# Causal scores in quarters: three 64 by 64 blocks per head in place of one 128 by 128, masked in two operations

## The chip, the cores and the metric

The kernel runs on one core of one Trainium2 chip. The core has TensorE (PE, matmuls; its weight loads are listed as PEld), VectorE (DVE), ScalarE (ACT), GpSimd (POOL) and SyncE (SP, which here issues the loads), and 16 DMA engines. The metric is the device time of one execution in microseconds, the median of several runs; lower is better.

## The reference

Retention attention (a linear attention with a decay per head) followed by a mixture of experts with one expert per token. Cut to what matters:

```python
# q, k, v: (4, 8, 768, 64)
gamma = 1.0 - 2.0 ** (-5.0 - np.arange(H))
for t in range(S):
    state = gamma * state + outer(k[t], v[t])        # per batch and head
    y[t] = scale * q[t] @ state
x = y as (B * S, H * D)                              # (3072, 512)
e_idx = argmax(x @ w_gate); gate_w = its softmax probability
eom = sigmoid(x @ w_output_gate)
out[token] = gate_w * eom[e_idx] * (relu(x @ w1[e_idx]) @ w2[e_idx])
```

Position t sees positions up to t only. Within a chunk of 128 positions the kernel computes this as scores of all keys with all queries, set to zero where the key is later than the query.

## The kernel before

The work has two parts. The first (about 0 to 155 us) is attention, routing and a scatter of the token rows to a list sorted by expert; the second runs the experts' two layers on TensorE to the end. The change lies in the first.

A sequence of 768 positions is cut into 6 chunks of 128; two chunks are a pair, so the 4 sequences give 12 pairs (`NPR`), j = 0 to 11, 3 to a sequence (`NJ`). The 8 heads are taken two by two: 4 groups (`NG`), and in each the even head lies on the lower 64 partitions and the odd head on the upper 64 (`LO`, `HI`, `half`). The order of the work is the order in which it is written: a loop over j (line 693) whose body calls small functions, each of which issues instructions on one or two engines; every engine takes its own in that order. For one pair the TensorE stages come in this order:

- `scores(j)` (line 336): for each of the two chunks c a PSUM tile `w` (two banks, one per head of a group; two such tiles take turns) receives keys by queries, 4 groups x 2 heads = 8 fp32 matmuls of 64 by 128 by 128. VectorE multiplies it with the 0/1 `mask` into `am` (line 346) in SBUF.
- `inter(j)` (L360): what the queries take from the state of earlier chunks, added up in the two banks `py`. Its matmuls lie on quarters of 64 by 64 of the array. For the first chunk of a sequence there is no state, and half of them fall away.
- `logits(j - 1)` (L394), `turn_k(j + 1)` (L311, transposes of the next keys into a `w` tile), `turn_l(j - 1)` (L402).
- `attend(j, 0)` (L367): values times `am` of the first chunk, into `py`; `weigh(j, 0)` (L374, VectorE) takes it out of PSUM. `state` (L383) updates the running state.
- `turn_q(j + 1)` (L329), `tokens(j - 1)` (L490), `counts(j - 1)` (L452 to L459), then `attend(j, 1)`, `weigh(j, 1)` and `state(j + 1, 0)`, and the next pair's scores.

Queries are stored with even positions of a chunk first and odd ones behind: column r x 64 + t of a query tile is position 2t + r (r = 0, 1). So positions 0 to 63, the early queries, are columns t = 0 to 31 of both halves, and the late ones t = 32 to 63. Keys are in plain order, partition p is position p.

In the profile each fp32 matmul shows as two LDWEIGHTS and two MATMUL records.

Of the kernel before, what the change touches and what calls it, by code (L numbers as in the profile page):

```python
# [10 lines left out]
F32 = mybir.dt.float32  # L11
# [5 lines left out]
ALU = mybir.AluOpType  # L17
# [15 lines left out]
def retention_moe_kernel(  # L33
# [14 lines left out]
    nc = tc.nc  # L48
    P = 128
# [5 lines left out]
    NG = H // 2  # L55
# [18 lines left out]
    mask = cpool.tile([P, 2, 64], F32, name="mask")  # L74
# [128 lines left out]
    with tc.manual_schedule(engines=None), ExitStack() as actx:  # L203
        ac = actx.enter_context(tc.tile_pool(name="ac", bufs=1))
        ap = actx.enter_context(tc.tile_pool(name="ap", bufs=2))
# [5 lines left out]
        qt, kt, vs, qr, ams, yts, sd, rt = {}, {}, {}, {}, {}, {}, {}, {}  # L211
        LO, HI = slice(0, 64), slice(64, 128)
        half = (LO, HI)

        def load2(which, src, tag, j, bufs):
            b, jb = divmod(j, NJ)
            t = ap.tile([P, 2, H, D], F32, name=tag, tag=tag, bufs=bufs)
            for c in range(2):
                r0 = (2 * jb + c) * P
                nc.sync.dma_start(t[:, c], src[b, :, r0:r0 + P, :].rearrange("h p d -> p h d"))  # L220
            which[j] = t

        def load_q(j):
            b, jb = divmod(j, NJ)
            t = ap.tile([P, H, 2, D], F32, name="qn", tag="qn", bufs=2)
            nc.sync.dma_start(t, q[b, :, jb * 2 * P:(jb + 1) * 2 * P, :].rearrange("h (p r) d -> p h r d", r=2))
            qn[j] = t
# [8 lines left out]
        gc = ac.tile([P, 2, NC, NG], F32, name="gc")  # L236
        wg = ac.tile([P, 2, NG, 32], F32, name="wg")
        gv = ac.tile([P, NC, H], F32, name="gv")

        load_q(0)  # L240
        load2(kn, k, "kn", 0, 3)
        load2(vn, v, "vn", 0, 2)
        nc.gpsimd.memset(wg, 0.0)
        nc.scalar.dma_start(gv, dec_v)
        load_q(1)
        for n, h in enumerate(half):
# [45 lines left out]
        def wide():  # L292
            return ps_w.tile([P, 2, 512], F32, name="w", tag="w")
# [24 lines left out]
        def turn_q(j, halved=False, tags=()):  # L318
# [14 lines left out]
                nc.scalar.copy(o.rearrange("p g c t -> p (g c t)"), w.rearrange("p b x -> p (b x)"))  # L333
            qt[j] = o

        def scores(j, between=None):
            for c in range(2):
                if c and between:
                    between()
                w = wide()  # L340
                for g in range(NG):
                    for hh in range(2):
                        nc.tensor.matmul(w[:, hh, g * P:(g + 1) * P], kt[j][half[hh], c, g], qt[j][half[hh], g, c],  # L343
                                         start=True, stop=True)
                a = ap.tile([P, 2, NG, P], F32, name="am", tag="am", bufs=2)
                nc.vector.tensor_tensor(  # L346
                    out=a.rearrange("p b g t -> p (b g) t"), in0=w.rearrange("p b (g t) -> p (b g) t", g=NG),
                    in1=mask.rearrange("p r t -> p (r t)").unsqueeze(1).broadcast_to([P, 2 * NG, P]), op=ALU.mult)
                ams[c] = a

        def open_y():
            rt["py"] = [ps_1.tile([P, 512], F32, name="py", tag=f"y{c}") for c in range(2)]
# [319 lines left out]
        load_pair(2)  # L672
        open_y()
        scores(0)
        prep_q(1, nc.vector)
        state(0, 0)
# [16 lines left out]
        for j in range(1, NPR - 1):  # L693
# [11 lines left out]
            if j >= 2 and j - 2 != EARLY:  # L705
                scatter(j - 2, 0)
            open_y()
            scores(j, (lambda: state(1, 0)) if j == 1 else None)
            if j - 1 in w_at:
                cast_weights(w_at[j - 1])  # L710
# [38 lines left out]
        j = NPR - 1  # L749
        scatter(j - 2, 0)  # L750
        scatter(j - 2, 1)
        open_y()
        scores(j)
        inter(j)
        logits(j - 1)
# [60 lines left out]
    with tc.manual_schedule(engines=None), ExitStack() as mctx:  # L816
# [197 lines left out]
        for s in range(NS + 1):  # L1014
            e, f = divmod(s, NF)
# [31 lines left out]
    with tc.If(odd > 0):  # L1047
        with ExitStack() as octx:
            oc = octx.enter_context(tc.tile_pool(name="oc", bufs=1))
            op = octx.enter_context(tc.tile_pool(name="op", bufs=2))  # L1050
# [49 lines left out]
            rows = oc.tile([P, 1], I32, name="rows")  # L1100
# [71 lines left out]
```

## Time and profile before

| | us |
|---|---|
| median of 3 runs (434.22 to 435.75) | 434.37 |
| the profiled execution's own time | 434.43 |
| its span, first to last instruction | 432.6 |
| TensorE busy | 413.7 (96%) |
| VectorE busy | 265.4 (61%) |
| ScalarE busy | 179.2 (41%) |
| GpSimd busy | 187.3 (43%) |
| the 24 mask operations, L346, 1219 ns each | 28.3 |

A row of a timeline gives the start, the length and the engine of instructions of the same kind that follow each other, then the line, the operation, what it writes and reads, and how many there are (x32). For matmuls "64*128" is the part of the array, rows by columns, and "64x128" what is streamed: partitions by columns. In brackets stands how long the engine stood idle before and what ended that. The end of a matmul is modelled, so the times between starts are the ones to use. A row of a window gives an engine's busy time in the stretch, its instructions in parentheses, and TensorE's granted clock as a share of full speed.

### The profile page before, as it was taken

What the parts mean: (1) busy time and instruction counts of PE and PEld (TensorE: products, weight loads), DVE (VectorE), ACT (ScalarE), POOL (GpSimd) and SP (SyncE); (2) the same over time, 40 slices, a digit from 0 to 9 for tenths busy, and PEclk for the clock granted to TensorE, in tenths of its full rate; (3) what the DMA queues carried; (4) which work ended last, traced back from release to release, by engine and by line L of the source; (5) the groups of instructions that cost most, each with busy time, mean ns of one, the idle gap of its engine ahead of it and who ended that gap; (6) DMA issues with size and microseconds to landing.
All of it is one profiled execution on the core that took longest, in us unless ns stands there. A gap on an engine that the chain in (4) does not pass through costs nothing.

```text
span 432.6 us, 10297 instructions
## 1 busy us (share of the span) xinstructions
PE 413.7 (96%) x3696; PEld 394.4 (91%) x3696; DVE 265.4 (61%) x701; ACT 179.2 (41%) x392; POOL 187.3 (43%) x255
## 2 busy tenths in 40 slices
PE   8799989999999999999999999999999999999990
PEld 5689878999979999999999999999999999999990
DVE  2667778677898757846456655664665756664110
ACT  2144454556546325544334443433444544441111
POOL 5446647666644216440025424524523533432522
PEclk9989999999999999999999999999999999999997
DMA  9999999999282498893394485558448549520102
GB/s 194 203 216 240 265 231 225 275 263 248 78 264 83 120 221 254 254 232 99 98 233 134 135 191 169 167 155 198 145 142 214 176 125 231 157 91 13 38 19 73
DMA packets 126878, 74.33 MB, mean 172 GB/s; under 512 B 56872, under 2 KB 115116, under 8 KB 126816
## 3 DMA queue, kind: packets, MB, share of 16 engines
q1 hardware_dynamic: 119888, 59.58, 54.9%
q0 software_dynamic: 5728, 13.93, 9.5%
q8 instruction: 31, 0.51, 0.5%
q10 hardware_dynamic: 1200, 0.06, 0.2%
q14 instruction: 31, 0.25, 0.2%
HBM read 59.62 MB, written 15.23 MB: 173 GB/s over the span
## 4 chain that ended last, share of the span: by engine, by line
PE 52%; issue 7%; POOL 3%; POOLq 0%; DVE 0%
PE h L875 26%; PE a L893 26%; POOL out_dram L178 3%; POOLq L178 0%; POOLq L1046 0%; DVE hl L880 0%; DVE a L1013 0%
## 5 line engine op out<-in xcount | busy, mean ns | idle before, releaser
L178 POOL DMA_INDIRECT out_dram<-ot,idi x83 | 87.2, 1050 | 150.4 <-ACT hh L879 123.2
L893 PE MATMUL a<-hh,whi 128*128 128x192 f32 (+7 forms) x256 | 85.6, 334 | 0.5 <-DVE a L1013 0.5
L893 PE MATMUL a<-hl,whi 128*128 128x192 f32 (+7 forms) x256 | 85.8, 335 | 0.1
L875 PE MATMUL h<-xh,whi 128*128 128x192 f32 (+7 forms) x256 | 85.7, 335 | 0.0
L875 PE MATMUL h<-xh,wlo 128*128 128x192 f32 (+7 forms) x256 | 85.7, 335 | 0.0
L875 PE MATMUL h<-xw,whi 128*128 128x192 f32 (+7 forms) x256 | 85.6, 335 | 0.0
L893 PE MATMUL a<-hh,wlo 128*128 128x192 f32 (+7 forms) x256 | 85.5, 334 | 0.0
L880 DVE SCALAR_TENSOR_TENSOR hl<-h,hh 128x192 fp32r<-128x192 f32 (+7 forms) x64 | 34.7, 544 | 63.9 <-ACT hh L879 63.8
L879 ACT ACTIVATE hh<-h 128x192 fp32r<-128x192 f32 (+7 forms) x64 | 30.8, 481 | 85.7 <-PE h L875 85.7
L165 DVE TENSOR_TENSOR wlo<-raw,whi 128x512 fp32r<-128x512 f32 x64 | 43.9, 686 | 30.1 <-ACT whi L160 28.7
L160 ACT CAST whi<-raw 128x512 fp32r<-128x512 f32 x64 | 39.6, 619 | 38.6 <-PE a L893 35.7
L893 PEld LDWEIGHTS a<-hh,whi 128*128 128x128 f32 x256 | 48.2, 188 | 1.1 <-ACT hh L879 0.7
L893 PEld LDWEIGHTS a<-hl,whi 128*128 128x128 f32 x256 | 48.2, 188 | 0.8 <-DVE hl L880 0.3
L875 PEld LDWEIGHTS h<-xh,wlo 128*128 128x128 f32 x256 | 48.2, 188 | 0.4
L875 PEld LDWEIGHTS h<-xh,whi 128*128 128x128 f32 x256 | 48.2, 188 | 0.4
L875 PEld LDWEIGHTS h<-xw,whi 128*128 128x128 f32 x256 | 48.2, 188 | 0.4
L893 PEld LDWEIGHTS a<-hh,wlo 128*128 128x128 f32 x256 | 48.2, 188 | 0.4
L166 DVE TENSOR_TENSOR wlo<-raw,whi 128x512 fp32r<-128x512 f32 x64 | 43.9, 685 | 0.3 <-ACT whi L160 0.3
L161 ACT CAST whi<-raw 128x512 fp32r<-128x512 f32 x64 | 39.5, 617 | 0.0
L346 DVE TENSOR_TENSOR am<-w,mask 128x1024 f32<-128x1024 f32 x24 | 28.3, 1219 | 6.7 <-PE w L343 6.6
L514 POOL DMA_INDIRECT srt<-row,posi x24 | 24.7, 1031 | 16.2 <-issue 5.2
L853 ACT CAST xh<-xt 128x416 fp32r<-128x416 f32 (+3 forms) x32 | 16.2, 510 | 37.0 <-DVE xt L852 37.0
(170 smaller groups left out, 610.9 us busy)
## 6 DMA issues: line engine op xcount, KB each, us to landing
raw<-in_moe_w_dram SPq DMA_DIRECT2D x128, 256.0 KB, 3.3
qn<-in_q_dram SPq DMA_DIRECT2D x12, 512.0 KB, 6.1
kn<-in_k_dram SPq DMA_DIRECT2D x24, 256.0 KB, 5.6
vn<-in_v_dram SPq DMA_DIRECT2D x24, 256.0 KB, 6.2
xl<-srt SPq DMA_DIRECT2D x12, 211.2 KB, 5.3
xl<-srt SPq DMA_DIRECT2D x12, 195.0 KB, 4.9
out_dram<-ot,idi POOLq DMA_INDIRECT x83, 2.6
xl<-srt SPq DMA_DIRECT2D x4, 227.5 KB, 6.9
```

The costliest lines, as they stand in the source:

```text
L160: nc.scalar.copy(hi[:, 0], raw[:, 0])
L161: nc.scalar.copy(perm(hi), r2)
L165: nc.vector.tensor_sub(lo[:, 0], raw[:, 0], hi[:, 0].bitcast(F32))
L166: nc.vector.tensor_sub(perm(lo), r2, perm(hi).bitcast(F32))
L178: st = nc.gpsimd.indirect_dma_start(out=dst, out_offset=bass.IndirectOffsetOnAxis(ap=idx, axis=0), in_=src, in_offset=None, bounds_check=n ...
L346: nc.vector.tensor_tensor(out=a.rearrange("p b g t -> p (b g) t"), in0=w.rearrange("p b (g t) -> p (b g) t", g=NG), in1=mask.rearrange("p ...
L514: st = nc.gpsimd.indirect_dma_start(out=srt, out_offset=bass.IndirectOffsetOnAxis(ap=posi[:, c:c + 1], axis=0), in_=row[:, c].rearrange("p ...
L853: nc.scalar.copy(xs[e][0][:, dc, w], tp[:, w])
L875: nc.tensor.matmul(ps[:, 0:C], l[:, 0, w], r[:, dc, 0:C], start=(n == 0), stop=(n == 3 * NDC - 1))
L879: relu = nc.scalar.activation(hh, ps[:, 0:C], AF.Relu)
L880: nc.vector.scalar_tensor_tensor(out=hl, in0=ps[:, 0:C], scalar=0.0, in1=hh.bitcast(F32), op0=ALU.max, op1=ALU.subtract)
L893: mm = nc.tensor.matmul(accs[d][:, 0:C], l[:, 1, w], r, start=(f == 0 and n == 0), stop=(f == NF - 1 and n == 2))
```

## The change

The score matrix of a chunk and head, 128 keys by 128 queries, is computed in three blocks of 64 by 64: early keys with late queries, late keys with late queries, early keys with early queries. The fourth, late keys with early queries, is all zero under the mask and is left out. The two `am` tiles become fixed tiles that are made once, and POOL sets that fourth block to zero in them at the start. The mask multiplies the late queries for all 128 keys in one operation and the early queries for the 64 early keys in a second one. All readers of `am` stay as they are.

```diff
--- before.py
+++ after.py
@@ -236,11 +236,15 @@
         gc = ac.tile([P, 2, NC, NG], F32, name="gc")
         wg = ac.tile([P, 2, NG, 32], F32, name="wg")
         gv = ac.tile([P, NC, H], F32, name="gv")
+        for c in range(2):
+            ams[c] = ac.tile([P, 2, NG, P], F32, name=f"am{c}")
 
         load_q(0)
         load2(kn, k, "kn", 0, 3)
         load2(vn, v, "vn", 0, 2)
         nc.gpsimd.memset(wg, 0.0)
+        for c in range(2):
+            nc.gpsimd.memset(ams[c].rearrange("p b g (r k t) -> p (b g) k r t", r=2, k=2)[HI, :, 0], 0.0)
         nc.scalar.dma_start(gv, dec_v)
         load_q(1)
         for n, h in enumerate(half):
@@ -333,20 +337,25 @@
                 nc.scalar.copy(o.rearrange("p g c t -> p (g c t)"), w.rearrange("p b x -> p (b x)"))
             qt[j] = o
 
+        def split(x):
+            return x.rearrange("p (r k t) -> p k r t", r=2, k=2)
+
         def scores(j, between=None):
             for c in range(2):
                 if c and between:
                     between()
                 w = wide()
                 for g in range(NG):
-                    for hh in range(2):
-                        nc.tensor.matmul(w[:, hh, g * P:(g + 1) * P], kt[j][half[hh], c, g], qt[j][half[hh], g, c],
-                                         start=True, stop=True)
-                a = ap.tile([P, 2, NG, P], F32, name="am", tag="am", bufs=2)
-                nc.vector.tensor_tensor(
-                    out=a.rearrange("p b g t -> p (b g) t"), in0=w.rearrange("p b (g t) -> p (b g) t", g=NG),
-                    in1=mask.rearrange("p r t -> p (r t)").unsqueeze(1).broadcast_to([P, 2 * NG, P]), op=ALU.mult)
-                ams[c] = a
+                    for lo, k in ((0, 1), (1, 1), (0, 0)):
+                        for hh in range(2):
+                            nc.tensor.matmul(split(w[half[lo], hh, g * P:(g + 1) * P])[:, k], kt[j][half[hh], c, g, half[lo]],
+                                             split(qt[j][half[hh], g, c])[:, k], start=True, stop=True, skip_group_check=True)
+                for k, rows in ((1, slice(0, P)), (0, LO)):
+                    nc.vector.tensor_tensor(
+                        out=ams[c].rearrange("p b g (r k t) -> p (b g) k r t", r=2, k=2)[rows, :, k],
+                        in0=w.rearrange("p b (g r k t) -> p (b g) k r t", g=NG, r=2, k=2)[rows, :, k],
+                        in1=mask.rearrange("p r (k t) -> p k r t", k=2)[rows, k].unsqueeze(1).broadcast_to([rows.stop, 2 * NG, 2, 32]),
+                        op=ALU.mult)
 
         def open_y():
             rt["py"] = [ps_1.tile([P, 512], F32, name="py", tag=f"y{c}") for c in range(2)]
```

On TensorE, in the pass of the loop for j = 3 from the end of the state update to the transposes of the next keys (`w` the score tile in PSUM, `st` the state, `py` the output banks, `kn` the keys; x7 counts rows alike). Before:

```order
L383 MATMUL st<-vs,kn 64x64 x7
L343 MATMUL w<-qt,kt 128x128 [waits Activation_49]
L343 MATMUL w<-qt,kt 128x128 x7
L343 MATMUL w<-qt,kt 128x128 [waits PE_49,Activation_49]
L343 MATMUL w<-qt,kt 128x128 x7
L360 MATMUL py<-qt,sd 64x128 [waits DVE_49,Activation_49]
L360 MATMUL py<-qt,sd 64x128 x7
L394 MATMUL misc<-yt,wg 32x128 x8
L311 MATMUL w<-ident,kn 128x128 [waits DMAHW6_49,DVE_49]
```

The same place with the change:

```order
L392 MATMUL st<-vs,kn 64x64 x7
L351 MATMUL w<-qt,kt 64x2x32 [waits Activation_49]
L351 MATMUL w<-qt,kt 64x2x32 x23
L351 MATMUL w<-qt,kt 64x2x32 [waits PE_49,Activation_49]
L351 MATMUL w<-qt,kt 64x2x32 x23
L369 MATMUL py<-qt,sd 64x128 [waits DVE_49,Activation_49]
L369 MATMUL py<-qt,sd 64x128 x7
L403 MATMUL misc<-yt,wg 32x128 x8
L315 MATMUL w<-ident,kn 128x128 [waits DMAHW6_49,DVE_49,PE_49]
```

16 score matmuls have become 48 smaller ones, in the same place; the first transpose of the next keys has one wait more, for TensorE itself (and so has that of the next queries).

On VectorE, the rows around the mask in the pass for j = 3 (`yt` is weigh's output, `lg` the logits). Before:

```order
L483 SCALAR_TENSOR_TENSOR posi<-pos,rank 128x2 [waits DVE_49]
L374 TENSOR_TENSOR yt<-py,gq 128x512 [waits PE_49]
L346 TENSOR_TENSOR am<-w,mask 128x1024 [waits PE_49] x2
L404 TENSOR_REDUCE lg<-misc 128x32 [waits PE_49]
L411 TENSOR_REDUCE m_621<-lg 128x2 [waits DVE_49]
```

With the change:

```order
L383 TENSOR_TENSOR yt<-py,gq 128x512 [waits PE_49]
L354 TENSOR_TENSOR am_120<-w,mask 128x16x32 [waits PE_49]
L354 TENSOR_TENSOR am_120<-w,mask 64x16x32
L354 TENSOR_TENSOR am_121<-w,mask 128x16x32 [waits PE_49]
L354 TENSOR_TENSOR am_121<-w,mask 64x16x32
L413 TENSOR_REDUCE lg<-misc 128x32 [waits PE_49]
```

Two operations have become four, between the same neighbours; each pair waits once.

## Rows read from the trace of the kernel before

**Rows 1.** The page: the span, and the engines' busy time.

```profile
span 432.6 us, 10297 instructions
...
PE 413.7 (96%) x3696; PEld 394.4 (91%) x3696; DVE 265.4 (61%) x701; ACT 179.2 (41%) x392; POOL 187.3 (43%) x255
```

**Rows 2.** Busy time by stretch, 70 to 90 us.

```profile
core 0: us, PE busy (x) PEld busy (x) DVE busy (x) ACT busy (x) POOL busy (x), PEclk, DMA share, GB/s
...
70.00:90.00 20.00, 20.00 (x337) 18.34 (x336) 15.05 (x61) 11.03 (x30) 13.15 (x22) 1.00 1.01 253
```

**Rows 3.** Timeline of TensorE, one pass of the loop.

```profile
62.05 1.09 PE L367 MATMUL py<-am,vs 128*64 128x128 f32 x16
62.97 0.64 PE L383 MATMUL st<-vs,kn 128*64 128x64 f32 x16
63.54 2.06 PE L343 MATMUL w<-qt,kt 64*128 64x128 f32 x32
65.52 1.10 PE L360 MATMUL py<-qt,sd 64*64 64x128 f32 x32
66.56 0.65 PE L394 MATMUL misc<-yt,wg 128*32 128x128 f32 x16
67.13 1.09 PE L311 MATMUL w<-ident,kn 128*128 128x128 f32 x8
...
68.26 1.09 PE L367 MATMUL py<-am,vs 128*64 128x128 f32 x16
69.29 1.09 PE L329 MATMUL w<-ident,qr 128*128 128x128 f32 x8
```

**Rows 4.** Timeline of TensorE, the next pass (first pair of a sequence).

```profile
74.72 1.09 PE L360 MATMUL py<-qt,sd 64*64 64x128 f32 x16
75.74 0.65 PE L394 MATMUL misc<-yt,wg 128*32 128x128 f32 x16
76.31 1.09 PE L311 MATMUL w<-ident,kn 128*128 128x128 f32 x8
```

**Rows 5.** Weight loads by line: ns shortest/median/longest, first and last start.

```profile
L394 PEld LDWEIGHTS misc<-yt,wg x192: 106/110/110, 25.6 to 130.6; 128*32 128x32 f32 x192
...
L360 PEld LDWEIGHTS py<-qt,sd x320: 129/133/133, 12.4 to 123.7; 64*64 64x64 f32 x160
...
L343 PEld LDWEIGHTS w<-qt,kt x384: 182/188/335, 8.8 to 122.7; 64*128 64x128 f32 x192
```

**Rows 6.** Timeline of TensorE behind the first pair.

```profile
18.78 1.09 PE L311 MATMUL w<-ident,kn 128*128 128x128 f32 x8 [2.82 <-DVE qt L331]
```

**Rows 7.** Timelines of VectorE, POOL and TensorE in the fifth pass.

```profile
51.83 3.11 DVE L658 TENSOR_SCALAR first<-io,base 128x8 f32<-128x8 f32 x1
...
51.88 1.17 POOL L283 COPY qr<-qn 128x512 f32<-128x512 f32 x2
53.01 1.90 POOL L275 TENSOR_TENSOR vs<-vn,gv 128x1024 f32<-128x1024 f32 x1
...
55.88 1.09 PE L360 MATMUL py<-qt,sd 64*64 64x128 f32 x28 [2.24 <-DVE yt L374]
```

**Rows 8.** Timeline of TensorE behind the last pair.

```profile
129.23 0.71 PE L604 MATMUL h<-xh,whi 128*128 128x256 f32 x4 [0.61 <-DVE se L442]
```

**Rows 9.** Timeline of VectorE: mask, and the logits behind it.

```profile
74.20 2.35 DVE L346 TENSOR_TENSOR am<-w,mask 128x1024 f32<-128x1024 f32 x2
77.55 0.23 DVE L404 TENSOR_REDUCE lg<-misc 128x32 f32<-128x64 f32 x1 [1.01 <-PE misc L402]
```

**Rows 10.** Instructions of line 374 (weigh).

```profile
L374 DVE TENSOR_TENSOR yt<-py,gq x24: 671/682/692, 15.4 to 129.5; 128x512 f32<-128x512 f32 x24
```

**Rows 11.** Waits, 20 to 130 us: total, times, longest.

```profile
DVE lg L404 <- PE misc L402: 11.9, 10, 1.6
```

**Rows 12.** Instructions of line 311 (next keys): the sequencer's semaphore steps.

```profile
L311 PEldq EVENT_SEMAPHORE  x12: 51/51/51, 15.0 to 114.2; - x12
```

**Rows 13.** Timeline of POOL at the start.

```profile
0.82 0.31 POOL L243 MEMSET wg<- 128x256 f32 x1 [0.29 <-POOLq L1156]
...
8.90 2.13 POOL L275 TENSOR_TENSOR vs<-vn,gv 128x512 f32<-128x512 f32 x2 [3.63 <-DMA vn<-in_v_dram]
```

## The prediction

> **What bounds the kernel now.** I read the engine totals first, then the busy time by stretch, then TensorE's timeline of one loop pass, and last the waits. TensorE is busy for 96% of the span [rows 1], and in the attention part, where the change lies, it has no gap at all: 20.00 of 20.00 us from 70 to 90 us, at the full clock [rows 2]. VectorE is busy for 15.05 us of that stretch. In that part what TensorE takes more or less is the kernel's time, as long as nobody else becomes late; so the question is what the score matmuls cost it.
>
> The timeline of TensorE [rows 3] is to be read by starts: a stage lasts from its first record to the next stage's. One fp32 matmul leaves two records. The form "64*128" says which part of the array a record uses (rows by columns of the array), "64x128" how much it streams (128 columns). Scores: 16 matmuls, 32 records, 63.54 to 65.52, **1.98 us**. The two heads of a group lie on the upper and lower 64 rows of the array, so two records run side by side, and 32 records are 16 rounds.
>
> That parts of the array work side by side is plain from inter (L360), whose matmuls lie on quarters of 64 by 64. In most passes it has 32 records on all four quarters and takes 65.52 to 66.56, 1.04 us; where the state of a sequence's first chunk is missing it has 16 records on two quarters and takes 74.72 to 75.74, 1.02 us [rows 3, 4]. Twice the records in the same time: the four quarters run together, and what counts is the rounds of the quarter that has most.
>
> A change of the split costs something too: attend (L367) takes 0.92 us where a stage of the same split follows (62.05 to 62.97) and 1.03 us where another does (68.26 to 69.29) [rows 3]. So **0.11 us per change of split**.
>
> **The change, part by part.**
> *Score matmuls.* Per group and head there were 128 keys by 128 queries in one matmul; now there are three of 64 by 64. Each goes to the quarter given by the head (rows) and the half of the keys (columns). Early keys meet both halves of the queries, late keys only the late ones. So the left half of the array gets two matmuls of 64 columns where it had one of 128, and the right half gets one. The left half streams 2 x 64 = 128 columns as before: what is left out frees the right half, and the right half does not set the end. Rounds of the left half per pair of chunks: 2 chunks x 4 groups x 2 blocks x 2 records = 32, of 64 columns. The nearest row for such a round is state (L383): 16 records of 64 columns, two side by side, 62.97 to 63.54 = 0.57 us, less 0.11 for the change of split behind it: 0.46 / 8 = **0.058 us per round** [rows 3]. 32 x 0.058 = 1.86 us. Scores now run in the same split as inter behind them, so one change of split per pass falls away. New stage 1.86 against 1.98: **-0.12 us per pass**. Bounds: no gain if a round takes 0.062 (1.98 / 32); at best -0.2, since half of one of inter's rounds, (1.04 - 0.11) / 8 / 2, is 0.058 us as well, and only the entry into inter, now in the split that stands, could give some 0.08 more.
>
> Could weight loads hold a round up? A load lasts 110 ns for 32 columns, 133 for 64 and 188 for 128 [rows 5], about 0.85 ns per column beyond a fixed part; 64 columns stream in 55 ns, under the 58 of a round, and in the old scores two loads of 128 ran side by side.
>
> *How many passes count.* Twelve pairs are scored. In the first, TensorE soon after waits 2.82 us for a copy that stands behind loads [rows 6]; there a gain or a loss under that is hidden. In the fifth it waits 2.24 us in inter for weigh [rows 7]: hidden too. In the last one VectorE, which weighs and masks without a pause, is what TensorE waits for (0.61 us, [rows 8]): no gain. Nine are left: 9 x -0.12 = **-1.08 us**.
>
> *Mask.* One operation of 1024 elements per partition, 1219 ns by the page's mean, becomes two of 512; weigh is such an operation from PSUM, 682 ns [rows 10]. That the second one has 64 partitions I count as no help. Back to back they overlap by some 0.09 us (2 x 1.219 would be 2.44, the row has 2.35 [rows 9]): 4 x 0.682 - 3 x 0.09 = 2.46 against 2.35, **+0.11 us** on VectorE per pass; at most 4 x 0.682 - 2.35 = +0.38 without the overlap, at least 0. It is hidden: VectorE then stands idle for 1.01 us before it reads the logits [rows 9], 11.9 us in ten passes [rows 11]. Turning the next keys needs the first buffer, masked by 74.20 + 1.2 = 75.4, and begins at 76.31 [rows 4, 9]. Only in the last pair is VectorE's chain on the path (above): **+0.11 us**.
>
> *New waits.* Turning the next keys and queries now also waits for TensorE's own score matmuls, since a quarter of the tile is written by none and read by none. Those ended at least 1.5 us before (65.52 against 67.13 [rows 3]). Price 0; at worst a semaphore step of 51 ns [rows 12] twice a pass, 9 x 0.1 = +0.9 us; I take 0, as the keys' stage has such steps already and starts on time.
>
> *Zeroing.* Two memsets on POOL at the start, 512 elements per partition each; one of 256 took 0.31 us [rows 13], so 1.2 us for both, at most. POOL idles 3.63 us there before its first values arrive [rows 13]. Price 0; with that cover gone 1.2 us.
>
> **Sum:** the profiled execution's time 434.43 us (span 432.6 and 1.8 around it; the median of the runs is 434.37) - 1.08 + 0.11 = **433.5 us**: no change that a measurement of this kernel can tell, which takes about 0.5%, 2.2 us.
>
> **Rivals.**
> *A. Too many records (slower).* 96 records must start in 1.86 us, one in 19.4 ns. The densest stages of the trace have one in 29 ns (inter 32 in 1.04 - 0.11 = 0.93 us, state 16 in 0.46 [rows 3]), and there the array's own rounds explain it. If something ahead of the array (issue, loads of weights, looking past records that wait for a busy quarter) allows no more, a pass pays from 1.98 / 96 = 20.6 ns on. At 24 ns, half way between needed and shown, scores take 2.30 us, +0.32 in nine passes: 434.4 + 2.9 + 0.1 = **437.4 us**. At the shown 29 ns, 2.78 us, +0.80 x 9: **441.7 us**. For it: nothing in the trace is denser. Against: in those stages the rate is just what full parts of the array need, so nothing else need have bounded them.
> [...]
> *B. The halves of the columns do not overlap (slower).* Then all three blocks of a group queue up: 48 rounds x 0.058 = 2.78 us, the time of A's far end, **441.7 us**. Against it: inter's four quarters.
> *C. A collision goes away (faster).* In the fifth pass a VectorE operation on 128x8 takes 3.11 us; it begins at 51.83, POOL's copies at 51.88, and it ends with POOL's last product (53.01 + 1.90) [rows 7]. It delays weigh, and TensorE waits 2.24 us. If the shifted order lets it finish before POOL begins, 433.5 - 2.3 = **431.2 us**. Against: both follow from the same counts on TensorE, so they should shift together.
>
> **How the numbers follow.** Forecast 0.62 (own range 432.4 to 434.9: the waits and the bounds above), A near 437 0.16, A's far end and B 0.14, C 0.07, rest 0.01. The range 432.2 to 439.0 leaves out the far end and C, 0.2. Slower by over 0.5%: 0.16 + 0.14 = 0.30; faster 0.08; same 0.62.
>
> **What would show it.** Right: scores of 96 records in 1.8 to 1.95 us; inter behind them without a pause for another split; the mask in four operations of about 0.68 us a pass; TensorE still without gaps from 70 to 90 us. Wrong: scores of 2.3 us or more (A, B; B if records of the right half start only when the left ones have ended), a wait before turning the keys, or a VectorE operation of 3 us gone (C).

## The result, and the profile after

The changed kernel takes **438.03 us** (median of 5 runs, 435.73 to 438.77) against 434.37 (434.14 to 435.75): ratio 1.0071, 95% interval 1.0049 to 1.0093. It is slower by 0.7%, 3.7 us. The forecast, no change, is wrong; the time lies in the range, on its slow side. The profiled execution was the best of the five: 435.73 us, span 434.0 against 432.6. So the profile holds 1.3 us of the 3.7; what the median execution loses beyond it was not profiled on this chip.

The page of the profile after: the span, the engines' busy time, and (section on DMA queues: packets, MB, share) the queue that carries instructions.

```profile
span 434.0 us, 11860 instructions
...
PE 413.4 (95%) x4464; PEld 394.8 (91%) x4464; DVE 266.1 (61%) x725; ACT 179.2 (41%) x392; POOL 188.7 (43%) x257
...
q8 instruction: 37, 0.61, 0.6%
...
L354 DVE TENSOR_TENSOR am<-w,mask 128x512 f32<-128x512 f32 (+1 forms) x48 | 29.7, 676 | 7.1 <-PE w L351 7.0
```

The same queue on the page before:

```profile
q8 instruction: 31, 0.51, 0.5%
```

TensorE is busy for as long as before ([rows 1]: 413.7 us), but with 768 MATMUL records more. Each has a weight load beside it, so that is 1536 instructions, and the queue q8 carried six packets more. Each of the packets has 16384 bytes in the trace's records (16 KB; 37 of them are the page's 0.61 MB), and 1536 / 6 = 256 instructions to a packet.

Timeline of TensorE, the pass of [rows 3]:

```profile
62.52 1.09 PE L376 MATMUL py<-am,vs 128*64 128x128 f32 x16
63.44 0.64 PE L392 MATMUL st<-vs,kn 128*64 128x64 f32 x16
64.00 2.02 PE L351 MATMUL w<-qt,kt 64*64 64x64 f32 x93
65.81 0.32 PE L369 MATMUL py<-qt,sd 64*64 64x128 f32 x1
...
65.92 1.04 PE L369 MATMUL py<-qt,sd 64*64 64x128 f32 x30
66.89 0.65 PE L403 MATMUL misc<-yt,wg 128*32 128x128 f32 x16
67.47 1.09 PE L315 MATMUL w<-ident,kn 128*128 128x128 f32 x8
```

Scores and inter together took 3.02 us before (63.54 to 66.56) and take 2.89 now (64.00 to 66.89): 0.13 less, as forecast. The first 93 score records start within 1.81 us, one in 19.5 ns, and inter follows without a pause.

Timeline of VectorE, the same pass and the last one:

```profile
65.20 2.47 DVE L354 TENSOR_TENSOR am<-w,mask 128x512 f32<-128x512 f32 x4 [0.83 <-PE w L351]
68.71 0.22 DVE L413 TENSOR_REDUCE lg<-misc 128x32 f32<-128x64 f32 x1 [1.03 <-PE misc L411]
...
123.72 2.46 DVE L354 TENSOR_TENSOR am<-w,mask 128x512 f32<-128x512 f32 x4
```

Four masks take 2.47 us (2.46 in the last pass) where two took 2.35 [rows 9]; the idle time before the logits is still there (1.03 against 1.01).

What is new shows first in the busy time from 70 to 90 us, where [rows 2] had no gap at all:

```profile
70.00:90.00 20.00, 19.40 (x457) 17.52 (x456) 14.50 (x62) 10.51 (x27) 13.08 (x22) 1.00 1.03 256
```

The missing 0.60 us, and more of its kind, in the timelines of TensorE and of its weight loads:

```profile
35.29 0.41 PE L403 MATMUL misc<-yt,wg 128*32 128x128 f32 x3
35.91 0.63 PE L403 MATMUL misc<-yt,wg 128*32 128x128 f32 x13 [0.22 <-issue]
...
88.05 0.33 PE L411 MATMUL misc<-ident,lt 128*128 128x128 f32 x1 [0.57 <-issue]
...
115.15 0.64 PE L403 MATMUL misc<-yt,wg 128*32 128x128 f32 x16 [0.23 <-issue]
...
123.85 1.04 PE L369 MATMUL py<-qt,sd 64*64 64x128 f32 x25
125.77 0.44 PE L369 MATMUL py<-qt,sd 64*64 64x128 f32 x6 [0.88 <-issue]
...
35.91 0.37 PEld L403 LDWEIGHTS misc<-yt,wg 128*32 128x32 f32 x13 [0.49 <-issue]
76.40 0.25 PEld L403 LDWEIGHTS misc<-yt,wg 128*32 128x32 f32 x9 [0.30 <-issue]
88.04 0.14 PEld L411 LDWEIGHTS misc<-ident,lt 128*128 128x128 f32 x1 [0.81 <-issue]
125.77 0.20 PEld L369 LDWEIGHTS py<-qt,sd 64*64 64x64 f32 x5 [1.13 <-issue]
```

In these five places TensorE stops, between two matmuls of one kind or between two stages, and the releaser is "issue": no semaphore and no engine. None of these stages was changed. The stop at 115.15 stands behind a branch of TensorE's sequencer (L723, 0.24 us from 114.85), and the kernel before waits there too (0.16 us in the profile of the second set). The other four are new. Counted from the first TensorE instruction of the trace (number 0), the first one behind each of these four has a number of the form 193 + 256k. Next to these numbers I put the landing of the packets of q8 (us; worked out from the trace's records; the matmul of the last row is one instruction ahead of the number):

```
number  line   started  packet landed  landing to start  the 256 ahead of it took
 1217   L403    35.91       34.40           1.51              3.46
 3009   L403    76.40       74.99           1.41              3.72
 3521   L411    88.04       86.54           1.50              4.67
 5313   L369   125.77      124.42           1.35              4.25
the other 16 numbers 193 + 256k up to 130 us:   1.64 to 7.16   2.97 to 10.58
the kernel before, all 14 up to 130 us:         3.42 to 9.56   6.49 to 12.43
```

At 4801 the 256 took 2.97 us only, but its packet had set off early and landed 2.50 us ahead: no stop. So the reading is: TensorE's instructions arrive in pieces of 256, and it stops at the end of a piece when the next has not been in for some 1.4 us (1.35 to 1.51 in the four stops).

How the sum comes out in this execution: the first matmul of the experts starts at 156.4 us, before at 154.6, so 1.8 later. Nine passes with 0.13 less give -1.2; the four idle times of the weight loads, 0.49 + 0.30 + 0.81 + 1.13, give 2.7; behind the first pair TensorE waits 3.2 us in place of the 2.82 of [rows 6], for a copy that stands behind loads (VectorE waits 1.85 us for one, to 15.07), 0.4. Sum +1.9. From there to the end it takes 0.4 less than before, so the span is 1.4 longer.

### The profile page after: what moved, and what is told of

Read it like the earlier page. It is cut to its first block, busy times and chain, and to the rows that moved or that the text cites. A ratio compares the mean times of both kernels' runs of the same rounds, so it can differ in the third digit from the quotient of the medians.

```text
span 434.0 us, 11860 instructions
## 1 busy us (share of the span) xinstructions
PE 413.4 (95%) x4464; PEld 394.8 (91%) x4464; DVE 266.1 (61%) x725; ACT 179.2 (41%) x392; POOL 188.7 (43%) x257
## 4 chain that ended last, share of the span: by engine, by line
PE 52%; issue 7%; POOL 3%; POOLq 0%; DVE 0%
PE h L884 26%; PE a L902 26%; POOL out_dram L178 3%; POOLq L178 0%; POOLq L1055 0%; DVE hl L889 0%; DVE a L1022 0%
## 5 line engine op out<-in xcount | busy, mean ns | idle before, releaser
L354 DVE TENSOR_TENSOR am<-w,mask 128x512 f32<-128x512 f32 (+1 forms) x48 | 29.7, 676 | 7.1 <-PE w L351 7.0
```

Of the source, the lines that this page charges most:

```text
L354: nc.vector.tensor_tensor(out=ams[c].rearrange("p b g (r k t) -> p (b g) k r t", r=2, k=2)[rows, :, k], in0=w.rearrange("p b (g r k t) -> ...
```

## The experiments

Theory F: the loss is these stops. 256 instructions that hold a scores stage pass in 3 to 5 us, and the next piece isn't there. Theory M: the loss comes from VectorE's mask and what waits behind it.

The runs went to five more chips. The kernel before took 434.9 and 435.1 us on two of them, as at first, and 443.9, 444.9 and 445.1 on three. Every ratio is to the kernel before on the same chip.

### First set: one part alone, and other numbers of blocks (before 443.9 us)

The changed kernel again, not edited:

> The changed kernel once more, to see in a second profile where the time goes. Theory F (fetch): the score matmuls themselves are no slower than forecast (scores and inter together 2.85 to 2.95 us a pass where 3.02 was), but TensorE now stands still in places where it waits for no semaphore, in the middle of inter or logits or before the transpose of the logits, because its next piece of instructions (the instruction queue q8, some 16 KB a packet, 37 packets where 31 were) is not there yet. Then this run has 2 to 5 such stops of 0.3 to 1.2 us, 1 to 4 us together, and a time of 436 to 439. Theory M (mask): VectorE's four mask operations hold TensorE up; then its stops end with a mask operation.

Measured: 452.05 us, ratio 1.0201 [1.0154, 1.0247]. On this chip it loses three times as much. The expectations of this set give times for the first chip; taken as ratios to its 434.4 us, F gave at most 1.011, 1.001, 1.020 and 1.003 for the four kernels, and every ratio measured here lies above that (the second and the fourth by their medians only, not by their intervals). What F leaves out on such a chip is in the fourth set.

The mask alone, with the scores matmul of before:

```diff
-                    for lo, k in ((0, 1), (1, 1), (0, 0)):
-                        for hh in range(2):
-                            nc.tensor.matmul(split(w[half[lo], hh, ...
+                    for hh in range(2):
+                        nc.tensor.matmul(w[:, hh, g * P:(g + 1) * P], kt[j][half[hh], c, g], qt[j][half[hh], g, c], ...
```

> The changed mask, the fixed tiles and the zeroing, but the 16 old score matmuls of 64 by 128 by 128 (the quarter that no mask operation reads is computed again). Theory F: no more instructions on TensorE, so the time of before within 0.5 us, 434.0 to 435.0, and no new stops. Theory M: most of the loss is here, 436.5 to 438.5.

Measured: 445.03 us, 1.0038 [0.9998, 1.0077]: a fifth of the loss, and not told from no change. M's 1.005 to 1.0095 overlaps this interval too, so this run alone does not exclude M.

Four blocks, with the mask of before in one operation:

```diff
-                    for lo, k in ((0, 1), (1, 1), (0, 0)):
+                    for lo, k in ((0, 1), (1, 1), (0, 0), (1, 0)):
...
```

> All four blocks of 64 by 64 are computed, so the right half of the array has as much to do as the left, 32 rounds, and the mask is one operation of 1024 again. 128 records a pass for the scores where the change has 96. Theory F: scores no longer than 1.95 us by themselves (the rounds are the same 32), but about 43 packets of instructions and more stops: 438.5 to 443, slower than the change. Theory M: the mask is the old one, so 433 to 434.5, faster than the change.

Measured: 457.16 us, 1.0309 [1.0252, 1.0366]. The slowest kernel of the set is the one with the old mask and the most records: M falls, unless several causes add up. In a pass without a stop it also shows what sets the stage:

```profile
34.28 2.09 PE L351 MATMUL w<-qt,kt 64*64 64x64 f32 x128
36.20 1.05 PE L366 MATMUL py<-qt,sd 64*64 64x128 f32 x32
37.18 0.64 PE L400 MATMUL misc<-yt,wg 128*32 128x128 f32 x16
```

Scores and inter take 2.90 us with 128 records, 2.89 with 96, and a record starts every 15 ns: with the same rounds on the left half of the array the stage lasts as long with 128 records as with 96.

Two blocks, with the mask of the change:

```diff
...
+                    for hh in range(2):
+                        nc.tensor.matmul(w[LO, hh, g * P:(g + 1) * P], kt[j][half[hh], c, g, LO], qt[j][half[hh], g, c], ...
+                    for hh in range(2):
+                        nc.tensor.matmul(split(w[HI, hh, g * P:(g + 1) * P])[:, 1], kt[j][half[hh], c, g, HI],
+                                         split(qt[j][half[hh], g, c])[:, 1], ...
```

> The same products left out, but the early keys meet all 128 queries in one matmul on the left half and the late keys the late queries in one of 64 columns on the right half: 64 records a pass where the change has 96, 16 rounds of 128 columns on the left half, masks as in the change. Theory F: scores 1.75 to 1.9 us, about 34 packets, fewer stops than the change: 433 to 435.5. Theory M: as slow as the change, 437 to 438.5.

Measured: 445.44 us, 1.0053 [1.0018, 1.0088]. The loss goes with the number of records: none more 0.4%, 384 more 0.5%, 768 more 2.0%, 1152 more 3.1%.

### Second set: the ends of the pieces moved (before 434.9 us)

The kernel before, for its profile on this chip:

> The kernel before, unchanged, for a profile of it on the chip on which the others of this set run. Both theories: ratio 1.000 within 0.3%. Theory F (TensorE's instructions arrive in pieces of 256, and a stretch that uses 256 of them in less than the time from asking for a piece to having it stops at the piece's end): on any chip this kernel's distance from the landing of a piece to the start of its first instruction stays over 2 us in the attention passes (3.4 us was the least in the first profile), so it has no stop of over 0.2 us at the instructions 193 + 256k. Theory M (the loss comes from VectorE's mask, which ends later): says nothing of it.

Measured: 434.64 us, 1.000 [0.9984, 1.0016]. From landing to start it is never under 3.60 us. Of TensorE's waits with "issue" from 20 to 130 us (total, times, longest) there is one, behind the branch:

```profile
PE misc L394 <- issue: 0.2, 1, 0.2
```

The changed kernel:

> The changed kernel on the same chip. Ratio 1.007 if the chip is like the first one, 1.02 if it is like the one of the set before. Theory F: stops of TensorE with no semaphore behind them at instructions 193 + 256k, each ending 1.35 to 1.6 us after the landing of a 16 KB packet of the instruction queue, 3 to 6 of them in the attention passes, 2 to 5 us in sum. Theory M: the stops, where there are some, end with the end of a VectorE instruction.

Measured: 438.28 us, 1.007 [1.0046, 1.0094]. The same view:

```profile
PE misc L403 <- issue: 1.9, 2, 1.7
PE w L351 <- issue: 0.6, 1, 0.6
PE py L369 <- issue: 0.4, 1, 0.4
```

Together 3.0 us before rounding, of which 0.2 (at L403) stand behind the branch. The stops are at 1217, 3009 and 5313 again and at 4289, inside scores (the one at 3009 shows in the weight loads alone); each ends 1.55 to 1.60 us behind a landing.

The changed kernel with everything half a piece later:

```diff
-        def idle(n):
+        def idle(n, m):
...
                 nc.tensor.matmul(pw[:, 0], wz[:, 0:P], wz, start=True, stop=True)
+            for _ in range(m):
+                nc.tensor.matmul(pw[0:32, 1, 0:32], wz[:, 0:32], wz[:, 0:32], start=True, stop=True)
...
-        idle(11)
+        idle(6, 69)
```

> The changed kernel with 64 short matmuls more in the warm-up (6 of 512 columns and 69 of 32, in place of 11 of 512), so that everything behind stands 128 TensorE instructions, half a piece, later; the arithmetic and the order are the same. Theory F: the ends of the pieces stay at instructions 193 + 256k and so fall 128 instructions earlier in the program: the stops at the logits behind the scores (before L403 and L411) are gone, and others come where a piece now ends within some 60 instructions behind a scores stage. Worked out from the profile of the changed kernel with 5 us from asking to having, the stops sum to 2.5 us where they were 5.6 by the same sum, so the time is 1 to 3 us under the changed kernel's on the same chip, ratio to it 0.993 to 0.998. Theory M, or any cause tied to a place in the program: the stops stay at the same instructions of the program, and the time is that of the changed kernel or up to 1 us over it (more instructions in the warm-up).

Measured: 435.87 us, 1.0029 [1.001, 1.0048]; against the changed kernel 435.87 / 438.28 = 0.9945, in the range given. The stops behind the scores at the logits are gone. The two longest ones are now at 449, in the first pair, where TensorE has 3 us of waiting to come anyway, and at 1729:

```profile
43.70 0.38 PE L371 MATMUL py<-qt,sd 64*64 64x128 f32 x3
44.47 0.87 PE L371 MATMUL py<-qt,sd 64*64 64x128 f32 x11 [0.39 <-issue]
```

The place in the program moved, the form 193 + 256k stayed.

The scores in two blocks:

> The scores in two blocks (early keys with all 128 queries in one matmul of 64 by 128, late keys with late queries in one of 64 by 64): the same work is left out, with 384 records more than before in place of 768. The mask is that of the change. Theory F: 256 instructions of a pass take longer than in the changed kernel, so at most one stop at a piece's end, and the time is within 0.5% of the kernel before, 0.5 to 1.5% under the changed kernel. Theory M: it has the changed kernel's mask and so its loss: ratio to the kernel before as for the changed kernel.

Measured: **433.99 us**, 0.9972 [0.9957, 0.9986]: the fastest version here, with the mask of the change. Its page:

```profile
PE 413.4 (95%) x4080; PEld 394.3 (91%) x4080; DVE 266.5 (62%) x725; ACT 179.1 (41%) x392; POOL 188.3 (43%) x257
```

and its busy time from 70 to 90 us:

```profile
70.00:90.00 20.00, 20.00 (x411) 18.41 (x411) 15.51 (x68) 11.74 (x32) 13.52 (x23) 1.00 1.00 255
```

No gap, and from landing to start never under 2.15 us. M falls here too: this kernel has the mask and not the loss. Its scores are also shorter by themselves:

```profile
83.84 0.33 PE L350 MATMUL w<-qt,kt 64*64 64x128 f32 x2
...
86.61 0.65 PE L405 MATMUL misc<-yt,wg 128*32 128x128 f32 x16
```

Scores and inter take 2.77 us, where the changed kernel takes 2.89 and the kernel before 3.02. In nine passes that is 1.1 of the 4.3 us by which it beats the changed kernel; fewer stops are not the whole of it. Both versions stream the same columns through the left half of the array; why 16 rounds of 128 columns take less than 32 of 64 was not tested.

### Third set: controls (before 444.9 us)

Theory W, a rival: the short matmuls of the warm-up gain the time by themselves. The changed kernel a whole piece later, `idle(2, 137)`:

> The changed kernel with 128 short matmuls more in the warm-up (2 of 512 columns and 137 of 32, in place of 11 of 512): everything behind stands 256 TensorE instructions later, one whole piece. Theory F (pieces of 256 instructions): the ends of the pieces fall on the same places of the program as in the changed kernel itself, so what the shift by half a piece gave is lost again: 437.5 to 439, ratio to the kernel before 1.006 to 1.01 on a chip like the last, and the stops lie at the instructions of the program at which the changed kernel has them (before L403, L411 and inside L369 of its numbering). A rival by which the short matmuls of the warm-up themselves gain the time (theory W): the gain is there again or doubles, 433.5 to 436.

Measured: 451.85 us, 1.0157 [1.0122, 1.0192]. It came to a chip of the other kind, so its time cannot be set beside those of the second set. Some of the places are those of the changed kernel (stops at 1473 = 1217 + 256 and 4545 = 4289 + 256); those before L411 and inside L369 were not there.

The kernel before with `idle(6, 69)`:

> The kernel before with the warm-up of the run shifted by half a piece (6 matmuls of 512 columns and 69 of 32). Theory F: it has no stop at a piece's end wherever these lie (256 instructions of it never take less than 6.5 us in the attention passes), so nothing changes: ratio 1.000 within 0.3%. Theory W: it gains what the changed kernel gained by it, ratio 0.993 to 0.996.

Measured: 444.81 us, 0.9998 [0.9966, 1.0031]. F expected this, and W did not. But on a chip of this kind the changed kernel gains nothing by the same shift either (fourth set), so W is not excluded by this run alone.

The mask alone again:

> The kernel before with the mask of the change (two operations, the left-out quarter zeroed once) and the scores matmuls of before: the mask's price by itself, on this chip. Theory F: ratio 0.999 to 1.003 (0.11 us of VectorE a pass, hidden in all but the last pass). Theory M (the mask is the loss): 1.007.

Measured: 443.95 us, 0.998 [0.9951, 1.001], a thousandth under the range of F; against M. Its interval ends under M's 1.007. The mask's price is zero as far as two runs can tell.

Two blocks with `idle(6, 69)`:

> The scores in two blocks with everything shifted by half a piece in the warm-up. Theory F: in two blocks a piece lasts over 4.8 us wherever the ends fall, so there is at most one stop of 0.5 us: 433.5 to 435, ratio 0.996 to 1.000, as without the shift within 0.3%. Theory W: 0.4 to 0.6% under the two blocks without it, 431.5 to 432.5.

Measured: 447.72 us, 1.0062 [1.0037, 1.0087]. A miss: outside both ranges, near the 1.0053 of two blocks without the shift on the other chip of this kind. So on these chips two blocks lose as well, and not at the ends of pieces.

### Fourth set: the three shifts together (before 445.1 us)

> The changed kernel, for the chip of this set. Ratio to the kernel before 1.007 on a chip where before takes 435 us, 1.016 to 1.02 where it takes 444. All theories alike.

> The changed kernel shifted by half a piece in the warm-up (6 matmuls of 512 columns, 69 of 32). Theory F (ends of pieces): 1.5 to 3 us under b4_after where before takes 435 us, 1 to 4 us under it where before takes 444. Theory W (the short matmuls of the warm-up gain by themselves): the same.

> The changed kernel shifted by a whole piece (2 matmuls of 512 columns, 137 of 32). Theory F: the ends of the pieces are on the places of b4_after again, so the time is b4_after's within 1 us, 1.5 us or more over b4_shift_128. Theory W: at or under b4_shift_128.

Measured: 451.04, 451.43 and 451.78 us; 1.0153 [1.0089, 1.0217], 1.0152 [1.0086, 1.0217], 1.017 [1.0107, 1.0233]. No difference, so the gain of 1 to 4 us that F gave for the half piece on such a chip did not come. In the three profiles TensorE's stops at ends of pieces between the first pair and 113 us are 1.2 us (at 1217), 0.7 (at 1729) and 0.4 (at 1473): here there is little that a shift could give back, less than the intervals can show. What the time goes into instead, in the waits of the unshifted kernel from 10 to 160 us:

```profile
PE w L351 <- issue: 4.0, 13, 0.5
```

and in its timeline of TensorE in one pass:

```profile
75.30 0.80 PE L351 MATMUL w<-qt,kt 64*64 64x64 f32 x28
76.30 1.46 PE L351 MATMUL w<-qt,kt 64*64 64x64 f32 x63 [0.20 <-issue]
```

On this chip TensorE stops in nearly every pass inside scores, some 55 instructions after their start, wherever the pieces end. The weight loads show it by the time from the first to the last start of a pass's scores. With three blocks that is 1.81 us without a stop; in the fourth to the tenth pass it is 0.45 to 0.66 us longer (more where the end of a piece falls into it). With two blocks it is 1.59 us and 0.23 to 0.44 longer, and with the old scores 1.68 us and no longer. So it is in all profiles of the three chips where before takes 444 us and more (around 115 and 127 us some more stops come with them, and the kernels with the old scores lose time there too). No profile of the other chips has it. It is a second kind of stop, in the kernels with more instructions alone; why these chips show it stays open.

Four blocks with the old mask:

> The scores in four blocks of 64 by 64, nothing left out, with the mask of before in one operation: 1152 matmul records more than before. Theory F: 256 instructions with the scores' 256 in them take about 2 us, so more of the pieces come late and by more: 3 to 8 us over the kernel before where it takes 435 us (1.007 to 1.018), 1.03 where it takes 444; the stops end 1.35 to 1.6 us after a packet's landing. Theory M (the mask): ratio 1.000 to 1.003, as the old mask is in it.

Measured: 456.42 us, 1.0289 [1.0221, 1.0357], as F gave it; five stops of 0.28 to 2.7 us at ends of pieces outside the first pair, besides those inside scores.

### Fifth set: half a piece against a whole one (before 435.1 us)

> The changed kernel shifted by a whole piece, 256 TensorE instructions, in the warm-up. Where before takes 435 us: Theory F (ends of pieces) ratio 1.006 to 1.009, as the changed kernel without a shift, 1.5 us or more over the shift by half a piece; Theory W (the short matmuls of the warm-up gain by themselves) 1.000 to 1.003. Where before takes 444 us: 1.015 to 1.017 by both, as in the last set.

> The changed kernel shifted by half a piece. Where before takes 435 us: ratio 1.002 to 1.004 by both theories. Where before takes 444 us: 1.015 by both.

Measured: **438.3 us**, 1.0093 [1.0063, 1.0123], against **435.11 us**, 1.0006 [0.9987, 1.0026] (this one just under what was expected, the other at the upper end). A whole piece loses again what half a piece gained, though it has 68 short matmuls more: W falls, and F stands on this chip. TensorE's waits from 20 to 130 us, of the whole piece:

```profile
PE py L371 <- issue: 1.2, 1, 1.2
PE misc L405 <- issue: 1.1, 2, 0.9
PE misc L413 <- issue: 0.6, 1, 0.6
...
PE w L353 <- issue: 0.4, 1, 0.4
```

and of half a piece:

```profile
PE py L371 <- issue: 0.2, 1, 0.2
```

Together 3.2 us before rounding, of which 0.2 (at L405) stand behind the branch, against 0.2; the median times differ by 3.2. The two profiled executions differ by 3.9, of which 1.0 arises in the first pair (the second pair's scores start at 22.1 and 21.1 us). The first stop of the whole piece is where the changed kernel's first one is, after three records of the logits:

```profile
36.32 0.41 PE L405 MATMUL misc<-yt,wg 128*32 128x128 f32 x3
37.63 0.64 PE L405 MATMUL misc<-yt,wg 128*32 128x128 f32 x13 [0.91 <-issue]
```

The other three are at 3777, 4545 and 5569: 3521, 4289 and 5313, where the changed kernel stopped in its two profiles above, each 256 higher. At 3265, 256 above its 3009, there is no stop here.

## Why the prediction was wrong

- **Score matmuls, -0.12 us per pass.** Right: -0.13. The rounds of the left half set the stage (four blocks, with as many rounds and more records, take 2.90 us with inter where three take 2.89), and inter follows in the same split without a pause.
- **Mask, +0.11 us, hidden.** Right: 2.47 against 2.35 us, and the mask alone cost nothing that two runs can tell (1.0038 [0.9998, 1.0077] and 0.998 [0.9951, 1.001]).
- **New waits and zeroing, 0.** Right: turning the next keys follows the logits without idle time (67.47), and the memsets took 1.0 us of POOL's time ahead of a wait that is still 2.1 us long.
- **Rival C.** It did not come: TensorE still waits 2.4 us for weigh in the fifth pass (2.24 in [rows 7]).
- **Rival B.** It did not come: scores would have taken 2.78 us.
- **Rival A.** It had the sign and nearly the time (437.4) but not the mechanism. Records were to start no faster than one in 24 ns, where a pass pays from 20.6 ns on; they start in 19.5. "Scores of 2.3 us or more" was the sign for it, and on this kind of chip scores stay at 1.9 (64.00 to 65.92); in four blocks a record started every 15 ns.

**The step that failed** is the sum under "The change, part by part": it priced the 768 records by array rounds, weight loads and starts, and had no term for bringing 1536 more instructions to TensorE. Rival A asked how fast records can start within the stage, not whether they are there. The missing term, TensorE's stops at ends of pieces, is 1.7 us in the first profile (2.7 by the weight loads), 2.8 in the second set and 3.0 in the fifth. Where they are nearly gone the rest of the sum comes out: in the profile with half a piece (fifth set) it is 133.3 us from the second pair's scores to the experts, in that of the kernel before 134.2 (second set, another chip at 435 us). That is 0.9 less, with one stop of 0.2 in it, where the sum has 1.0 less. "TensorE still without gaps from 70 to 90 us" was the sign that failed.

Most of it was to be had. The instruction queue is on the page before with 31 packets. In the attention part no packet set off before TensorE had started the instruction about 280 ahead of the piece's first (at most 286, in all profiles). Counted from 290 ahead, it set off after 2.2 us (median of all profiles) and took 1.2 us. That much the trace before shows as well; that the piece is in use 1.2 to 1.6 us later at the earliest, only the stops show. Together, as an estimate, it is about 5 us from asking to having, with a wide spread, as packets set off 0.1 to 9.6 us behind that mark. The kernel before takes 6.5 us or more for 256 instructions, and its pieces were in 3.4 us or more ahead of use. The change puts 192 of them into 1.9 us.

## What to carry to other kernels

Count instructions as a cost of their own: where smaller tiles multiply the matmuls, look for the shortest time in which 256 TensorE instructions pass, and compare it with the time from asking for a piece to having it (some 5 us here, by the estimate above). Stops with "issue" as releaser in a stage that nobody touched, at instruction numbers 256 apart, are its mark, and adding half a piece of cheap instructions at the start is a quick way to test for it, where no other stops cover the effect as they did on three chips here. Of two splits that leave out the same products take the one with fewer instructions: two blocks were 1% under three on the chip without the second kind of stop (433.99 against 438.28 us), about a quarter of it in the scores themselves.

## What had not been expected of the hardware

- TensorE's instructions come in pieces of 256 (1536 more of them in six more packets, the stops at 193 + 256k), and a late piece stopped it for 0.2 to 2.7 us.
- The cost of the same instructions differs by the chip: the changed kernel loses 0.7% on chips where before takes 435 us, 1.5 and 2.0% where it takes 444 to 445.
- The densest start of records seen is one in 15 ns, in four blocks of 64 by 64 on four quarters; in the changed kernel, with three, it is one in 19.5 ns.
- In the second set TensorE's granted clock fell to 0.50 of full speed in the fifth pass of the changed kernel, after a wait of 2.38 us for weigh; the kernel before kept 1.00 after 2.24 us. Busy time by stretch (the column behind POOL is the granted clock), of the changed kernel:

```profile
58.00:59.00 1.00, 1.00 (x24) 0.97 (x16) 1.00 (x3) 0.00 (x0) 0.00 (x0) 0.50 0.96 273
59.00:60.00 1.00, 1.00 (x20) 0.59 (x16) 0.64 (x2) 0.00 (x0) 0.00 (x0) 0.50 0.75 192
```

and of the kernel before:

```profile
57.00:58.00 1.00, 1.00 (x32) 0.66 (x24) 1.00 (x2) 0.00 (x0) 0.00 (x0) 1.00 0.59 146
```

  From the end of that wait to the next queries it took 5.71 us in place of 4.22 (57.40 to 63.11, 56.44 to 60.66), 1.5 us of the 3.7 by which the experts began later in that pair of profiles. The shift by half a piece and the two blocks had this fall in their profiles of the same set, where they were 2.4 and 4.3 us faster, and the first profile of the changed kernel and both of the fifth set did not. Elsewhere the whole piece of the third set alone has it there, and none of the five profiles with the old scores. So it does not go with the stops, and comes in some executions of the new scores only; what decides it stays open. It may be part of what the first median lost beyond its profile, but no run shows that.
